# The first reciprocal spread on ScalarE, and nine dummy matmuls for nineteen

## The chip, the cores and the metric

The kernel runs on one core of a Trainium2 chip. A core has five engines that each work through their own queue of instructions in order: TensorE (PE, matrix products; its weight loads are listed as PEld), VectorE (DVE), ScalarE (ACT), GpSimd (POOL) and SyncE (SP), which here only issues DMAs. An instruction that waits holds up everything behind it in its queue. The metric is the device time of one execution in microseconds; smaller is better.

## The reference

Two layers, one after the other. The first is a polynomial-sketch linear attention on q, k and v of 4 batches, 4 heads, 1088 positions and 32 features; the second is a gated feed-forward layer on its output, seen as 4352 tokens of 128 features.

```python
def phi(x):                                  # r = 8, so 64 features
    a = einsum('rd,bhsd->bhsr', S1, x)
    b = einsum('rd,bhsd->bhsr', S2, x)
    return einsum('bhsi,bhsj->bhsij', a, b).reshape(..., r * r)
q_p, k_p = phi(q), phi(k)
kv  = einsum('bhsf,bhsd->bhfd', k_p, v)
z   = sum(k_p, axis=2)
num = einsum('bhsf,bhfd->bhsd', q_p, kv)
den = einsum('bhsf,bhf->bhs', q_p, z)[..., None] + 1e-06
x   = (num / den) in the layout [tokens, heads * features]
out = (relu(x @ w_gate) * (x @ w_val)) @ w_out      # 128 -> 1536 -> 128
```

## The kernel before

The program is a list of operations (`P.add(engine, name, function, inputs)`), made by classes: `K` for k and v of one batch, `First` for the first 512 columns of q of batch 0, `Q` for the other pieces of q, and `F` for one unit of the feed-forward layer. The order is written out by hand: `START` holds a position for each operation, in the order in which the operations were added, and `Plan.run` issues them sorted by it. Each engine thus gets its own queue in that order, and waits only where an input is not ready or a buffer (a PSUM bank by `BANKS`) is not free. `WARM` names operations ahead of which some dummy matmuls are put into PE's queue, 128x128 products of a tile of zeros into PSUM bank 7 (L1007 in the profile).

Batch 0 is worked first so that feed-forward units can start early. For it, `First` handles q in two halves, y = 0 and 1, with a shortcut for the division: the denominator of each (position, head) is built on its own, and its reciprocal is laid out transposed so that it can be multiplied onto the numerator when that leaves PSUM. The steps of one half, with the lines of the profile:

- `f bw` (L672, DVE) multiplies the two factors of the denominator into fbw, `f red` (L614, DVE) sums them, `f rd` (L616, DVE) takes the reciprocal into frd, 8 values per partition.
- `f rx` (L618, DVE in the kernel before) copies each of those 8 values 32 times, 128x8 to 128x256 in fp32, into frx.
- `f rT` (L679, PE) transposes frx by two products with an identity, `f rTe` (L623, ACT) copies the result from PSUM to frT.
- `f phi` (L687, POOL) makes the q features, `f tr` (L696, PE) transposes them, `f pt` (L633, ACT) copies them to fpt, `f num` (L700, PE) multiplies them with bd, the masked kv sum.
- `f xd` (L707, DVE) multiplies numerator and frT into xT, which is what the feed-forward units read.

Around them stand, in the same queues: `kphi` (L534, DVE or POOL), the k features; `kv` (L559, PE) with its evacuation `kve` (L565, DVE) into bd; `w` (L519, PE) with `wc` (L523, ACT); `L` (L379, ACT), a small copy; `cw` (L311, ACT), the casts of the first third of the three weight matrices, that of the gate weights, `cw g0`, first; `qt1 0 4` (L979, DVE), a transpose of the rest of q of batch 0; `gate` (L385, ACT), a one-element cast whose end lets SP issue the loads of the next batches (`ld k1`, L389, first); and on POOL the DMA issues for the other thirds of the weights (L305).

In issue order, the queues near the change are these. DVE: f rd 0, f bw 1, f rx 0, f red 1, f rd 1, kphi 0 6, f rx 1, qt1 0 4, kve 0, f xd 0. ACT: L, cw g0, f rTe 0, wc 0, f pt 0, gate, cw v0, f pt 1, f rTe 1. PE: f csk 1, nineteen dummies, f rT 0, kv 0 0, w 0, f tr 0, four more kv, f rT 1, f tr 1, f num 0, then a score product of the next piece, f num 1 and the first units. POOL: f phi 0, the loads wg2 and wg1, f phi 1, the loads wv2 and wv1.

A feed-forward unit is two products of xT with gate and value weights (L908, PE), a relu out of PSUM (L913, ACT), their product (L923, DVE, or L917 on ACT and L928 on POOL), and the product with the output weights (L936, PE).

Of the kernel before, what the change touches and what calls it, by code (L numbers as in the profile page):

```python
# [27 lines left out]
FILL = 'DVE'  # L28
RINGS = [['ld s1', 'ld s2', 'ld k01', 'ld v000', 'ld v001', 'ld v002', 'ld v003', 'ld v010', 'ld v011', 'ld v012', 'ld v013'], ['mz', 'kt1 0 0'], ['fills', 'kt1 0 0'], ['zero', 'fills'], ['ld k00', 'ld q00', 'table'], ['vc 0 0', 'gate'], ['zero', 'mz'], ['zero', 'sel'], ['zero', 'masks'], ['id32', 's1r', 'ld wg1', 'ld wv1'], ['kphi 0 8', 'ld wo1', 'ld wg2', 'ld wv2', 'ld wo2'], ['ld v013', 'ld wg0', 'ld wv0', 'ld q01'], ['ld wv0', 'ld k1']]
Q0E = 'ACT'  # L30
RXE = 'DVE'
START = [
# [67 lines left out]
]  # L100
WARM = {34: 29, 63: 2, 143: 14, 147: 1, 152: 19}


class Lease:
# [15 lines left out]
class Plan:  # L120
# [10 lines left out]
    def run(self, warm):  # L131
        assert not START or len(START) == len(self.ops)
        order = sorted(self.ops, key=lambda o: (START[o.seq] if START else 0, o.seq))
        for o in order:
            if o.seq in WARM:
                warm(WARM[o.seq])
            o.fn()
# [3 lines left out]
def kernel(  # L141
# [37 lines left out]
    def sb(shape, dt, name):  # L179
        return const.tile(shape, dt, name=name)  # L180

    P = Plan()

    def bank(l, i=0):
        return PS[:, l.banks[i]]
# [393 lines left out]
    cp = {"ACT": nc.scalar.copy, "DVE": nc.vector.tensor_copy, "POOL": nc.gpsimd.tensor_copy}  # L579

    class First:


        def __init__(self, kk, qt1):
            self.kk, n = kk, 4
            self.n = n
            self.ab = sb([128, 2, n, 2, 16], FP32, "fab")
            self.aT = sb([128, n * 128], FP32, "faT")
            self.bw = fbw
            self.dn, self.rd = sb([128, n * H], FP32, "fdn"), sb([128, n * H], FP32, "frd")  # L590
            self.rx = sb([128, n, H, D], FP32, "frx")
            self.rT = sb([128, n * 128], FP32, "frT")
            self.qp = sb([128, n, 2, 128], FP16, "fqp")
            self.pt = sb([128, n, 2, 128], FP16, "fpt")
            rts, t2s = [], []
            for y in range(2):
                la = Lease(P, 2)
                s1 = P.add("PE", f"f sk {y}", lambda y=y, la=la: self.sk(la, y), [qt1[y], ws_op],
                           take=[la])
                t2 = P.add("DVE", f"f t2 {y}", lambda y=y, la=la: self.t2(la, y), [s1],  # L600
                           drop=[la])
                t2s.append(t2)
                lat, lc, lr = Lease(P), Lease(P), Lease(P)
                at = P.add("PE", f"f aT {y}", lambda y=y, l=lat: self.at(l, y), [qt1[y], s1r_op],
                           take=[lat])
                ate = P.add("ACT", f"f aTe {y}", lambda y=y, l=lat: nc.scalar.copy(
                    out=self.aT[:, 256 * y:256 * y + 256], in_=bank(l)[:, 0:256]), [at, ftab],
                    drop=[lat])
                cs = P.add("PE", f"f csk {y}", lambda y=y, l=lc: self.csk(l, y),
                           [kk.zc_op, ate], take=[lc])  # L610
                o1 = P.add("DVE", f"f bw {y}", lambda y=y, l=lc: self.mul(l, y), [t2, cs, f2],
                           drop=[lc])
                h = slice(2 * H * y, 2 * H * y + 2 * H)
                o2 = P.add("DVE", f"f red {y}", lambda h=h: nc.vector.tensor_reduce(  # L614
                    out=self.dn[:, h], in_=self.bw[:, h], axis=AX.X, op=ALU.add), [o1])
                o3 = P.add("DVE", f"f rd {y}", lambda h=h: nc.vector.reciprocal(  # L616
                    out=self.rd[:, h], in_=self.dn[:, h]), [o2])
                rx = P.add(RXE, f"f rx {y}", lambda h=h, y=y: cp[RXE](  # L618
                    out=self.rx[:, 2 * y:2 * y + 2].rearrange("p x h d -> p (x h) d"),
                    in_=self.rd[:, h, None].to_broadcast([128, 2 * H, D])), [o3])  # L620
                rt = P.add("PE", f"f rT {y}", lambda y=y, l=lr: self.rt(l, y), [rx, fid32],
                           take=[lr])
                rts.append(P.add("ACT", f"f rTe {y}", lambda y=y, l=lr: nc.scalar.copy(  # L623
                    out=self.rT[:, 256 * y:256 * y + 256], in_=bank(l)[:, 0:256]), [rt],
                    drop=[lr]))
            self.x_ops = []
            for y in range(2):
                x = slice(2 * y, 2 * y + 2)
                lt, ln = Lease(P), Lease(P)
                phi = P.add("POOL", f"f phi {y}", lambda x=x: self.phi(x), [t2s[y]])  # L630
                tr = P.add("PE", f"f tr {y}", lambda x=x, lt=lt: self.tr(lt, x), [phi, fident],
                           take=[lt])
                pt = P.add("ACT", f"f pt {y}", lambda x=x, lt=lt: nc.scalar.copy(  # L633
                    out=self.pt[:, x].rearrange("f x g t -> f (x g t)"),
                    in_=bank(lt).bitcast(FP16)[:, 0:512]), [tr], drop=[lt])
                num = P.add("PE", f"f num {y}", lambda x=x, ln=ln: self.num(ln, x),
                            [pt, kk.kve], take=[ln])
                self.x_ops.append(P.add(
                    "DVE", f"f xd {y}", lambda y=y, ln=ln: self.xd(ln, y), [num, rts[y]], drop=[ln]))
# [405 lines left out]
```

## Time and profile before

| | |
|---|---|
| median of 3 runs | 105.07 us (104.68 to 108.16) |
| the profiled execution's own time | 104.74 us |
| its span, first to last instruction | 103.0 us |
| mean granted PE clock | 0.994 of full speed |
| PE / DVE / ACT / POOL busy | 97.0 / 85.7 / 82.3 / 60.5 us |
| dummy matmuls (L1007) | 65, of which 19 ahead of the first transposes |

All times in a trace are counted from the span's start. A line of the timeline gives start, length, engine, source line, operation, output <- input with shape and count, and in brackets how long the engine had stood idle before and what ended that. Neighbouring instructions of one group are merged into one line, whose length is from the first start to the last end. A line of the chain gives start, length and what. A row of a group of one tile gives shortest, median and longest duration in ns, then the first and last start.

### The profile page before, as it was taken

The numbers are of one execution on the slowest core, as the hardware profiler recorded it, in microseconds if no ns is written. First come the engines' busy times: TensorE is split into PE (matmuls) and PEld (weight loads), VectorE is DVE, ScalarE is ACT, GpSimd is POOL, SyncE is SP. The second block draws the span as 40 slices with busy tenths as digits, with TensorE's granted clock in tenths as the row PEclk, the third lists the DMA queues.
The fourth block names the chain that finished last, engine by engine and source line by source line (L and its number), as shares of the span: only waits on it lengthen the run. The fifth ranks groups of instructions, "written<-read, shape, count | busy, mean of one in ns | idle before, by whom it ended". The sixth has DMA issues, their size and how long they took to land.

```text
span 103.0 us, 3182 instructions
## 1 busy us (share of the span) xinstructions
PE 97.0 (94%) x1233; PEld 70.2 (68%) x1233; DVE 85.7 (83%) x191; ACT 82.3 (80%) x165; POOL 60.5 (59%) x71
## 2 busy tenths in 40 slices
PE   6999999987999999999999999999999999999950
PEld 6978889845779865556675666656676666678930
DVE  4587969999999898999999887998969895986740
ACT  3437289999797776999988898788998999899920
POOL 2029955978999999995994987108800030264400
PEclk9999999999999999999999999999999999999997
DMA  2988689999994495205530040420513423004131
GB/s 55 350 215 309 101 136 317 354 287 250 227 265 97 118 86 127 54 16 159 149 87 10 0 102 6 102 51 0 127 33 78 108 51 76 6 0 107 46 102 51
DMA packets 14800, 12.40 MB, mean 120 GB/s; under 512 B 8257, under 2 KB 12353, under 8 KB 14785
## 3 DMA queue, kind: packets, MB, share of 16 engines
q1 hardware_dynamic: 13392, 10.70, 40.3%
q0 software_dynamic: 864, 0.79, 5.3%
q10 hardware_dynamic: 528, 0.72, 2.3%
q8 instruction: 9, 0.15, 0.6%
q14 instruction: 7, 0.05, 0.2%
HBM read 9.05 MB, written 2.23 MB: 110 GB/s over the span
## 4 chain that ended last, share of the span: by engine, by line
PE 83%; DVE 11%; issue 1%; ACT 0%; DVEq 0%; POOL 0%
PE ps L908 39%; PE ps L936 22%; PE ps L1007 5%; DVE ht L923 5%; PE ps L559 2%; PE ps L772 2%; PE ps L840 2%; PE ps L492 2%; PE ps L506 2%; DVE kT L483 2%; PE ps L679 1%; PE ps L519 1%; PE ps L666 1%; PE ps L658 1%; DVE frx L618 1%
## 5 line engine op out<-in xcount | busy, mean ns | idle before, releaser
L923 DVE TENSOR_TENSOR ht<-g_sb,ps 128x512 f16<-128x512 f16 (+1 forms) x88 | 55.7, 671 | 7.5 <-PE ps L908 5.1
L913 ACT ACTIVATE g_sb<-ps 128x512 f16<-128x512 f32 x102 | 55.4, 606 | 6.6 <-PE ps L908 6.1
L936 PEld LDWEIGHTS <-ht 128*128 128x128 f16 x408 | 28.2, 98 | 11.1 <-issue 1.8
L908 PE MATMUL ps<-xT,wv 128*128 128x512 f16 (+1 forms) x132 | 35.6, 332 | 0.1
L936 PE MATMUL ps<-wo,ht 128*128 128x128 f16 x408 | 34.6, 219 | 0.0
L908 PE MATMUL ps<-xT,wg 128*128 128x512 f16 (+1 forms) x132 | 34.4, 331 | 0.0
L928 POOL TENSOR_TENSOR ht<-g_sb,v_sb 128x512 f16<-128x512 f16 x15 | 17.2, 1157 | 18.0 <-ACT g_sb L913 14.2
L908 PEld LDWEIGHTS <-wg 128*128 128x128 f16 x132 | 14.1, 114 | 4.3 <-issue 0.8
L534 POOL TENSOR_TENSOR kp<-kab 128x512 f16<-128x512 f32 (+2 forms) x14 | 15.6, 1132 | 2.2 <-DVE kab L498 2.2
L908 PEld LDWEIGHTS <-wv 128*128 128x128 f16 x132 | 13.8, 115 | 4.3 <-issue 1.4
L813 POOL TENSOR_TENSOR qqp<-qan,qabc 128x1024 f16<-128x1024 f32 (+1 forms) x9 | 14.9, 1660 | 0.4
L917 ACT CAST v_sb<-ps 128x512 f16<-128x512 f32 x15 | 9.2, 615 | 0.3
L807 POOL TENSOR_TENSOR qan<-qabc,qrd 128x128 f32<-128x128 f32 (+1 forms) x9 | 3.4, 372 | 7.8 <-DVE qrd L803 7.8
L1007 PE MATMUL ps<-zero 128*128 128x128 f16 x65 | 6.6, 280 | 1.0 <-DVE zero L287 1.0
L1007 PEld LDWEIGHTS <-zero 128*128 128x128 f16 x65 | 5.8, 132 | 1.3 <-DVE zero L287 1.0
L785 DVE STREAM_TRANSPOSE qabc<-ps 128x128 f32<-128x128 f32 (+1 forms) x12 | 5.5, 493 | 0.5 <-PE ps L772 0.4
L979 DVE STREAM_TRANSPOSE qT<-q_sb 128x544 f32<-128x544 f32 (+2 forms) x9 | 5.8, 656 | 0.0
L943 ACT ACTIVATE o_sb<-ps 128x512 f32<-128x512 f32 (+1 forms) x10 | 5.2, 520 | 0.7 <-PE ps L936 0.6
L793 POOL TENSOR_TENSOR bw<-qabc 128x128 f32<-128x128 f32 (+1 forms) x9 | 3.6, 408 | 3.6 <-DVE qabc L785 3.5
L853 ACT CAST xT<-ps 128x512 f16<-128x512 f32 (+1 forms) x9 | 4.8, 535 | 0.6 <-PE ps L840 0.4
L483 DVE STREAM_TRANSPOSE kT<-k_sb 128x544 f32<-128x544 f32 x6 | 4.2, 719 | 0.0
L548 ACT CAST v<-v 128x576 f16<-128x576 f32 x6 | 4.0, 692 | 0.1
(92 smaller groups left out, 78.4 us busy)
## 6 DMA issues: line engine op xcount, KB each, us to landing
k_sb<-in_k_dram SPq DMA_DIRECT2D x3, 544.0 KB
q_sb<-in_q_dram SPq DMA_DIRECT2D x3, 544.0 KB, 10.6
out_dram<-o_sb SPq DMA_DIRECT2D x22, 64.0 KB, 1.7
v<-in_v_dram SPq DMA_DIRECT2D x6, 144.0 KB, 10.0
v<-in_v_dram SPq DMA_DIRECT2D x6, 128.0 KB, 7.8
out_dram<-o_sb SPq DMA_DIRECT2D x16, 32.0 KB, 2.1
v<-in_v_dram SPq DMA_DIRECT2D x6, 64.0 KB, 3.3
k_sb<-in_k_dram SPq DMA_DIRECT2D x1, 288.0 KB, 4.3
```

The costliest lines, as they stand in the source:

```text
L483: nc.vector.transpose(self.kT[:, r], k_sb[self.b][:, r])
L534: eng.tensor_tensor(out=self.kp[:, lo:hi].rearrange("p x g (i a c) -> p (x g i) a c", i=2, a=R), in0=a[:, :, :, None].to_broadcast([128, n ...
L785: nc.vector.transpose(self.abc[:, lo:lo + m, 2 * i2:2 * i2 + 2].rearrange("p x h f -> p h x f"), pair(ls[i2])[:, :, lo * 32:(lo + m) * 32] ...
L813: nc.gpsimd.tensor_tensor(out=self.qp[:, lo:hi].rearrange("p x g (i a c) -> p (x g i) a c", i=2, a=R), in0=self.an[:, lo * H:hi * H, :, No ...
L908: nc.tensor.matmul(bank(l)[:, y * self.W:(y + 1) * self.W], w[:, j // 4, :, j % 4], x, start=True, stop=True, skip_group_check=True)
L913: nc.scalar.activation(out=self.gs, in_=bank(l), func=ACTF.Relu)
L917: nc.scalar.copy(out=self.vs, in_=bank(l))
L923: nc.vector.tensor_tensor(out=self.ht[:, t], in0=self.gs[:, t], in1=bank(l)[:, t], op=ALU.mult)
L928: nc.gpsimd.tensor_tensor(out=self.ht, in0=self.gs, in1=self.vs, op=ALU.mult)
L936: nc.tensor.matmul(o[:, s], self.ht[:, i * 128:(i + 1) * 128], wo[:, j // 4, j % 4], start=(j == 0 and s == 0), stop=(j == NJ - 1), skip_g ...
L979: nc.vector.transpose(qT[b][:, lo:hi], q_sb[b][:, lo:hi])
L1007: nc.tensor.matmul(PS[:, 7, 0:128], zero, zero, start=True, stop=True, skip_group_check=True)
```

## The change

The first of the two `f rx` copies, y = 0, is given to ACT; the second stays on DVE. In the issue order it takes the place just ahead of `cw g0` on ACT's queue; the positions between its new and its old place each move back by one. Ahead of `f rT 0` stand nine dummies in place of nineteen. The computation is the same.

```diff
-RXE = 'DVE'
+RXE = ['ACT', 'DVE']
 START = [ ...
-    2, 4, 1, 8, 6, 43, 10, 12, 13, 15, 17, 22, 28, 31, 3, 9, 0, 14, 34, 64, 40, 89, 20, 103, 71,
-    93, 51, 66, 87, 125, ...
+    2, 4, 1, 8, 6, 43, 10, 12, 13, 15, 17, 22, 28, 31, 3, 9, 0, 14, 34, 65, 40, 89, 20, 103, 71,
+    93, 51, 67, 87, 125, ...
...
-    35, 42, 48, 54, 58, 60, 63, 67, 69, 76, 57, 62, 38, 44, 59, 65, 68, ...
+    35, 42, 48, 54, 58, 60, 63, 64, 69, 76, 57, 62, 38, 44, 59, 66, 68, ...
...
-WARM = {34: 29, 63: 2, 143: 14, 147: 1, 152: 19}
+WARM = {34: 29, 63: 2, 143: 14, 147: 1, 152: 9}
...
-                rx = P.add(RXE, f"f rx {y}", lambda h=h, y=y: cp[RXE](
+                rx = P.add(RXE[y], f"f rx {y}", lambda h=h, y=y: cp[RXE[y]](
                     out=self.rx[:, 2 * y:2 * y + 2].rearrange("p x h d -> p (x h) d"),
                     in_=self.rd[:, h, None].to_broadcast([128, 2 * H, D])), [o3])
```

Of the four moved positions, 64 to 65 is `cw g0`, 66 to 67 is `ld wg2` on POOL, 65 to 66 is `f bw 1`, and 67 to 64 is `f rx 0`. The order within every other queue stays as it was.

4 rows, old and new, of the table START are left out of this document.

## The prediction

> **What bounds the kernel now.** The page comes first: the busy shares, and the chain of work that ended last.
>
> ```profile
> span 103.0 us, 3182 instructions
> PE 97.0 (94%) x1233; PEld 70.2 (68%) x1233; DVE 85.7 (83%) x191; ACT 82.3 (80%) x165; POOL 60.5 (59%) x71
> PE 83%; DVE 11%; issue 1%; ACT 0%; DVEq 0%; POOL 0%
> ```
>
> TensorE (PE) is busy for 94% of the span and carries 83% of the chain. That is an average over stages, so the second view is the table by stretches (columns: length, then busy time of PE, PEld, DVE, ACT and POOL with instruction counts, the granted PE clock, the DMA share, GB/s).
>
> ```profile
> 11.00:12.00 1.00, 1.00 (x19) 0.86 (x16) 0.99 (x2) 0.47 (x1) 0.99 (x3) 1.00 0.60 112
> ...
> 16.00:18.00 2.00, 2.00 (x20) 1.93 (x19) 1.85 (x9) 1.87 (x5) 1.30 (x4) 1.00 1.03 350
> 24.00:27.00 3.00, 2.56 (x62) 1.63 (x61) 3.00 (x8) 2.93 (x8) 2.92 (x3) 1.00 1.10 223
> 27.00:40.00 13.00, 13.00 (x234) 10.28 (x218) 12.35 (x25) 10.38 (x21) 12.58 (x13) 1.00 0.78 156
> 80.00:95.00 15.00, 15.00 (x149) 10.65 (x148) 12.14 (x20) 14.41 (x29) 4.58 (x4) 1.00 0.23 57
> ```
>
> From 27 us on PE has no gap: what is left to do there takes its own time, and a stage that starts earlier ends earlier by as much. Between 16 and 27 us DVE is as good as full. The change sits at 11 to 12 us, ahead of both, where PE looks full only because dummies fill it. The third view is the chain in order of time.
>
> ```profile
> 11.01 0.22 DVE fbw L672
> 11.23 0.96 DVE frx L618
> 12.23 0.71 PE ps L679 x4
> ...
> 14.02 0.64 PE ps L679 x4
> ...
> 14.89 0.25 PE ps L700 x2
> 15.23 0.40 DVE xT L707
> ```
>
> The copy that is moved (L618, 0.96 us of it) is on the path that sets the end; the dummies beside it are not. Behind it the PE queue runs through without a break to the product that is the first block of xT. The last view is the timeline around it.
>
> ```profile
> 9.82 0.26 ACT L379 COPY L<-ps 128x128 f32<-128x128 f32 x1
> ...
> 10.81 1.12 POOL L305 DMA_DIRECT2D wg<-in_moe_w_gate_dram  x2
> 10.81 0.16 DVE L616 RECIPROCAL frd<-fdn 128x8 f32<-128x8 f32 x1
> 10.81 1.23 PE L1007 MATMUL ps<-zero 128*128 128x128 f16 x19
> 11.01 0.22 DVE L672 TENSOR_TENSOR fbw<-fab,ps 128x64 f32<-128x64 f32 x1
> 11.15 1.03 DVE L618 COPY frx<-frd 128x256 f32<-128x256 f32 x1
> 11.53 0.62 ACT L311 CAST wg<-qabc 128x512 f16<-128x512 f32 x1 [1.45 <-DMA qabc<-in_moe_w_gate_dram]
> 11.94 1.17 POOL L687 TENSOR_TENSOR fqp<-fab 128x512 f16<-128x512 f32 x1
> 12.10 0.21 DVE L614 TENSOR_REDUCE fdn<-fbw 128x8 f32<-128x72 f32 x1
> 12.23 0.52 PEld L679 LDWEIGHTS ps<-id,frx 128*128 128x128 f32 x4 [0.38 <-DVE frx L618]
> ...
> 12.47 0.64 DVE L534 TENSOR_TENSOR kp<-kab,ps 128x512 f16<-128x512 f32 x1
> ...
> 12.98 0.37 ACT L623 COPY frT<-ps 128x256 f32<-128x256 f32 x1 [0.84 <-PE ps L679]
> ...
> 13.02 0.29 DVE L618 COPY frx<-frd 128x256 f32<-128x256 f32 x1
> 13.06 1.12 POOL L305 DMA_DIRECT2D wv<-in_moe_w_val_dram  x2
> 13.23 0.77 DVE L979 STREAM_TRANSPOSE qT<-q_sb 128x576 f32<-128x576 f32 x1
> ```
>
> Two things are to be seen. The two copies of L618 have the same shape, and the first takes 1.03 us, the second 0.29. The first lies under POOL's two DMA issues (10.81 to 11.93) and ends 0.25 us after them. And ACT stands idle from 10.08 to 11.53, waiting for the gate weights to land.
>
> **The change part by part.** *The copy on ACT.* Its input is ready when the reciprocal ends, 10.81 + 0.16 = 10.97. For the hand-over I take the 0.05 us by which PE followed the copy in the trace (11.15 + 1.03 = 12.18, and 12.23), so it starts at 11.02. The trace has no ACT copy of this source; the two rows below and the 1.03 us bound it.
>
> ```profile
> L606 ACT COPY faT<-ps x2: 372/372/373, 8.1 to 8.6; 128x256 f32<-128x256 f32 x2
> 14.12 0.61 ACT L311 CAST wv<-qabc 128x512 f16<-128x512 f32 x1
> ```
>
> ACT copies 128x256 from PSUM in 0.37 us; the same copy took 1.03 on DVE. I take 0.37, since the ACT cast at 11.53 lay partly under POOL's DMA issue and took the 0.62 us that its fellow at 14.12 takes. The copy ends at 11.39, inside ACT's idle time: the cast of the gate weights, which waits for its DMA, still starts at 11.53, and the insertion costs nothing. At 1.03 us the copy would end at 12.05 and that cast at 12.67.
>
> *The dummies.* Nineteen take 1.23 us; nine take 9/19 of it, 0.58, and end at 11.39. With nineteen the queue would hold the transposes until 12.04, so the move alone would bring 0.19 us; the two edits need each other. With the hand-over of 0.05 behind ACT's 11.39 the transposes start at 11.44, call it 11.45. **At this place 12.23 - 11.45 = 0.78 us is won.**
>
> *What ACT does next.* The evacuation at L623 started 0.75 us after the transposes, so at 12.20, behind the cast's end at 12.15: it moves by the same 0.78, as do the copies behind it.
>
> *What DVE does next.* Without the copy the second half's reduction follows its product as the first half's did, about 0.25 us after 11.01: 11.26 for 12.10. The reciprocal, the kp product and the second copy keep their distances (12.47 and 13.02 less 12.10), so the product ends at 12.27 and the second copy asks at 12.18. That is where the forecast divides. In the trace of before this copy met POOL's multiply (11.94 to 13.11) only in its last 0.09 us; now it would meet 0.9 us of it. Either it runs at once, 0.29 us to 12.47, or it waits as the first one did and ends 0.25 after POOL, at 13.11 + 0.25 = 13.36. I take the second, because the only copy of this form that began well inside a POOL operation was held to its end.
>
> The Trainium skill, SBUF — State Buffer, section "SBUF: two separate sides", says that DVE and GpSimd share one port pair under an exclusive lock, and that an fp32 copy from SBUF to SBUF asks for it and is shut out for the whole instruction of the other. The 1.03 us beside 0.29 agree with it for DMA issues; no run yet shows it for the multiply. By that rule POOL, first at 11.94, keeps the second copy out, and the time is that of the forecast; without it, that of the first rival.
>
> *How far that takes the gain back.* The rows that follow, from the timeline, carry the next steps; the last is the time from issue to landing of the two wv loads.
>
> ```profile
> 13.95 0.71 PE L679 MATMUL ps<-id,frx 128*128 128x128 f32 x4
> 14.03 0.18 ACT L385 CAST k_sb<-zero 1x1 f32<-1x1 f16 x1
> 14.06 0.29 DVE L565 TENSOR_TENSOR bd<-ps,maskg 128x128 f16<-128x128 f32 x1
> 14.24 0.80 SPq L389 DMA_DIRECT2D k_sb<-in_k_dram  x2
> 14.82 0.30 PE L700 MATMUL ps<-fpt,bd 128*64 128x256 f16 x2
> 17.64 0.38 PE L908 MATMUL ps<-xT,wv 128*128 128x256 f16 x2
> DMA to landing us min/median/max: 3.0/3.3/3.7
> ```
>
> From the first transposes to the second PE had 13.95 - 12.23 = 1.72 us of work without a gap: if the second copy is free, the second ones would start at 13.17; held, at 13.41. Behind the held copy the DVE queue is where it was: the qT transpose about 13.28 to 14.05, then the evacuation of kv, 14.06 before, now 14.07, 0.29 long, to 14.36. With 0.05 the products of L700 can start at 14.41; before it was PE's own queue that let them start at 14.82.
>
> So **0.41 us are left at L700**, and xT, the first gate product and all behind them move by that. The sum is made against the profiled execution, 104.74 us of its own (span 103.0 and 1.74 around it): 104.74 - 0.41 = 104.33. The runs shown have their median at 105.07, 0.33 above it, and the lowest at 104.68; I give **104.35** and keep the scatter for the range.
>
> *What the moved ACT queue triggers.* The tiny cast at 14.03 opens SP's queue: k of the next batch is issued at 14.24 behind it, and would be at 13.46. These 544 KB then meet the last two weight loads of POOL's queue, issued at 13.06 and after and landed 3.0 to 3.7 us later (last row). The first is needed by PE at 17.64, at 17.23 when all is 0.41 earlier; it lands by 13.06 + 3.7 = 16.76, so 0.47 us are in hand.
>
> **Rivals.** *The second copy runs free.* Then the qT transpose behind it waits only for its q.
>
> ```profile
> 7.60 0.44 SPq L265 DMA_DIRECT2D q_sb<-in_q_dram  x1
> q_sb<-in_q_dram SPq DMA_DIRECT2D x1, 288.0 KB, 5.3
> ```
>
> That lands at 7.60 + 5.3 = 12.9; the transpose ends at 12.9 + 0.77 = 13.67 and the kv evacuation about 0.3 later, at 13.97. PE's order is then the limit throughout: L700 at 14.82 - 0.78 = 14.04. Time 103.96. For it: the 0.29 us. Against it: that copy had all but outlived POOL's work.
>
> *The gain is lost on the way.* Either the ACT copy takes 1.03 us like its fellow (transposes at 12.10, 0.13 won, 104.61), or the earlier k pushes the weight load back by the whole 0.78 us that it comes forward, to 17.54: PE then stands 0.31 us, 0.10 is left, 104.64. Call both 104.6.
>
> *Slower than before.* The same load waits out the whole transfer of k: 544 KB at the 350 GB/s of the stretch from 16 to 18 us are 1.56 us, it lands at 18.32, and PE's queue stands there 0.68 us longer than before: 105.42. It decides from a push of 0.88 us (past 17.64). Against it: k was already under way from 14.24 while these loads were landing.
>
> *The clock falls.* Ten dummies less could let the granted clock drop; if PE ran at half of it from the first transposes to the end of the first L700 (12.23 to 15.12 before), those 2.9 us would cost 2.9 more, about 107.2. Against it: the gap ahead of the transposes shrinks (0.2 us before, about 0.06 after), and the clock is 1.00 in every stretch above. The Trainium skill, TensorE: Matmul & The Clock Gate, Part 1, puts an idle window of about 3.4 us ahead of a drop, which the gap is far from.
>
> **How the numbers follow.** Forecast 0.48 (104.35); second copy free 0.22 (103.96); gain lost 0.16 (104.6); slower by the load 0.10 (105.4); clock 0.04 (107). Below: the lowest run less the larger gain is 104.68 - 0.78 = 103.90; 0.2 for half the scatter of 104.68 to 105.07 gives 103.7. Above: the slower case, 105.4, taken to 105.5, which is also the median shown with its own scatter on top. Within 2% (2.1 us) is what a measurement of this kernel can't tell from no change: all cases but the clock lie in it. Faster by over 2% would need 2.1 us where 0.78 is the most: 0.02. Slower by over 2%: the clock, and a little for a median that falls among runs like the 108.16 shown, 0.06. Same: 0.92.
>
> **What would show it.** Right: an ACT copy into frx at about 11.0 of 0.37 us, the gate cast still at 11.5, nine dummies ending at 11.4, L679 first at 11.45, the second L618 drawn out to about 1.1 us and ended at 13.3, L700 at 14.4, PE without a gap from 26.6. A second L618 of 0.3 us with L700 at 14.0 speaks for the first rival; an ACT copy near 1 us, or a PE wait before the products with wv at 17 us, for the second and third; a granted clock under 1.00 at 12 to 15 us for the last. The prediction is wrong if stages behind 16 us, which I let move as one, change their waits.

## The result, and the profile after

| | before | after |
|---|---|---|
| median of 20 runs | 104.94 us (104.28 to 110.98) | 104.92 us (103.57 to 108.52) |
| ratio of undisturbed executions, 95% | | 0.9935 (0.9906 to 0.9965) |
| the profiled execution's own time | 104.74 us | 103.83 us |
| its span | 103.0 us | 102.1 us |

By the ratio 0.65% is won, 0.68 us of 104.74 (0.37 to 0.98): faster beyond its interval, and within the 2% called the same. The medians show none of it: the ratio keeps of each kernel only the executions within 1.5% of its own fastest, ten of twenty of the changed kernel and fifteen of the kernel before; with one line of 105.84 us for both, fifteen of each, the means are 104.53 and 104.84 us. That would be a gain of 0.3%, so its size leans on where the line is drawn. A second set of the changed kernel, at the end of the experiments, gave 0.9914. The forecast was 104.35 in a range of 103.7 to 105.5, with 0.41 us won.

The page of the changed kernel, its busy shares and its chain:

```profile
span 102.1 us, 3160 instructions
PE 96.4 (94%) x1223; PEld 69.4 (68%) x1223; DVE 85.4 (84%) x190; ACT 82.5 (81%) x166; POOL 60.3 (59%) x71
PE 85%; DVE 9%; issue 1%; ACT 0%; POOL 0%; DVEq 0%
```

Ten matmuls and one DVE instruction fewer, one ACT instruction more; DVE's share of the chain fell from 11% to 9%. The timeline around the change:

```profile
10.68 0.16 DVE L616 RECIPROCAL frd<-fdn 128x8 f32<-128x8 f32 x1
10.68 1.12 POOL L305 DMA_DIRECT2D wg<-in_moe_w_gate_dram  x2
10.68 0.67 PE L1007 MATMUL ps<-zero 128*128 128x128 f16 x9
10.87 0.40 ACT L618 COPY frx<-frd 128x256 f32<-128x256 f32 x1 [0.90 <-DVE frd L616]
...
11.18 0.61 ACT L311 CAST wg<-qabc 128x512 f16<-128x512 f32 x1
11.33 0.52 PEld L679 LDWEIGHTS ps<-id,frx 128*128 128x128 f32 x4 [0.15 <-ACT frx L618]
...
11.81 1.09 POOL L687 TENSOR_TENSOR fqp<-fab 128x512 f16<-128x512 f32 x1
...
12.08 0.98 DVE L618 COPY frx<-frd 128x256 f32<-128x256 f32 x1
...
12.98 0.76 DVE L979 STREAM_TRANSPOSE qT<-q_sb 128x576 f32<-128x576 f32 x1
...
13.12 0.71 PE L679 MATMUL ps<-id,frx 128*128 128x128 f32 x4
...
13.33 0.80 SPq L389 DMA_DIRECT2D k_sb<-in_k_dram  x2
...
13.68 0.24 DVE L565 TENSOR_TENSOR bd<-ps,maskg 128x128 f16<-128x128 f32 x1
...
13.98 0.30 PE L700 MATMUL ps<-fpt,bd 128*64 128x256 f16 x2
```

The copy runs on ACT in 0.40 us. The second one, left on DVE, is now the long one: 0.98 us under POOL's multiply, where it took 0.29 before. Read all of this against the start of the first reciprocal (L616), since the first loads land a little differently in every execution, and with them everything moves: the reciprocal starts at 10.81 before and at 10.68 after.

| us after the first reciprocal's start | before | forecast | after |
|---|---|---|---|
| first L679 | 1.42 | 0.64 | 0.65 |
| second L618, start to end | 2.21 to 2.50 | 1.37 to 2.55 | 1.40 to 2.39 |
| second L679 | 3.14 | 2.60 | 2.44 |
| kv evacuation L565, start | 3.25 | 3.26 | 3.00 |
| first L700 | 4.01 | 3.60 | 3.30 |

0.71 us are won at L700. Behind it the kernel is what it was: from the start of L700 to the end of the span 103.0 - 14.82 = 88.2 us before and 102.1 - 13.98 = 88.1 after. So 0.91 us between the two profiled executions is 0.13 of an earlier reciprocal, 0.71 of the change and 0.07 of the rest. The table by stretches of the changed kernel (columns as in the prediction) shows the same PE stage without a gap from 27 us on:

```profile
12.00:13.00 1.00, 1.00 (x25) 0.94 (x22) 1.00 (x3) 0.88 (x3) 1.00 (x2) 1.00 0.86 109
24.00:27.00 3.00, 2.62 (x60) 1.89 (x60) 2.95 (x7) 2.82 (x7) 3.00 (x4) 1.00 1.05 237
27.00:40.00 13.00, 12.99 (x217) 10.09 (x215) 12.16 (x25) 9.77 (x20) 12.73 (x13) 1.00 0.74 147
```

One wait is new. The view of the tile wv in the changed kernel has its two loads landed 4.1 to 5.5 us after their issue, not 3.0 to 3.7:

```profile
DMA to landing us min/median/max: 4.1/4.8/5.5
```

and in the timeline PE stood for one of them:

```profile
16.98 0.14 PEld L908 LDWEIGHTS <-wv 128*128 128x128 f16 x2 [0.28 <-DMA wv<-in_moe_w_val_dram]
```

It cost nothing at the end. DVE's first product of a unit (ht, L923) started 2.91 us after L700 in both profiles (17.73 - 14.82, and 16.89 - 13.98), and four of them later the first transpose of k (L483) started 5.34 us after L700 in both (20.16 - 14.82, and 19.32 - 13.98).

### The profile page after: what moved, and what is told of

Same layout as the page of the kernel before. It is cut to its first block, busy times and chain, and to the rows that moved or that the text cites. A ratio compares the mean times of both kernels' runs of the same rounds, so it can differ in the third digit from the quotient of the medians.

```text
span 102.1 us, 3160 instructions
## 1 busy us (share of the span) xinstructions
PE 96.4 (94%) x1223; PEld 69.4 (68%) x1223; DVE 85.4 (84%) x190; ACT 82.5 (81%) x166; POOL 60.3 (59%) x71
## 4 chain that ended last, share of the span: by engine, by line
PE 85%; DVE 9%; issue 1%; ACT 0%; POOL 0%; DVEq 0%
PE ps L908 39%; PE ps L936 23%; PE ps L1007 5%; DVE ht L923 4%; PE ps L559 2%; PE ps L772 2%; PE ps L840 2%; PE ps L492 2%; PE ps L506 2%; DVE kT L483 2%; PE ps L679 1%; PE ps L519 1%; PE ps L658 1%; PE ps L666 1%; DVE qabc L785 1%
## 5 line engine op out<-in xcount | busy, mean ns | idle before, releaser
L923 DVE TENSOR_TENSOR ht<-g_sb,ps 128x512 f16<-128x512 f16 (+1 forms) x88 | 55.6, 671 | 7.5 <-PE ps L908 4.9
L928 POOL TENSOR_TENSOR ht<-g_sb,v_sb 128x512 f16<-128x512 f16 x15 | 17.2, 1156 | 17.9 <-ACT g_sb L913 14.2
L1007 PE MATMUL ps<-zero 128*128 128x128 f16 x55 | 5.9, 287 | 1.0 <-DVE zero L287 1.0
L1007 PEld LDWEIGHTS <-zero 128*128 128x128 f16 x55 | 5.1, 136 | 1.3 <-DVE zero L287 1.0
L483 DVE STREAM_TRANSPOSE kT<-k_sb 128x544 f32<-128x544 f32 x6 | 4.2, 719 | 0.0
```

What stands on the lines that cost most here:

```text
L483: nc.vector.transpose(self.kT[:, r], k_sb[self.b][:, r])
L923: nc.vector.tensor_tensor(out=self.ht[:, t], in0=self.gs[:, t], in1=bank(l)[:, t], op=ALU.mult)
L928: nc.gpsimd.tensor_tensor(out=self.ht, in0=self.gs, in1=self.vs, op=ALU.mult)
L1007: nc.tensor.matmul(PS[:, 7, 0:128], zero, zero, start=True, stop=True, skip_group_check=True)
```

## Experiments

Theory: the first copy was long because DVE was kept out while POOL issued its loads; the dummies were the next bound; the stages behind move as one. A time such as R + 0.65 is in us after the start of the first reciprocal of that execution. The ratios are to the kernel before on the same chip.

**The move alone.** Nineteen dummies again.

```diff
-WARM = {..., 147: 1, 152: 9}
+WARM = {..., 147: 1, 152: 19}
```

> The first copy on ACT, but nineteen dummies as before. Theory (the copy was held behind POOL, and the dummies would hold the transposes next): the ACT copy again 0.40 us, but the first L679 starts only when the dummies end, 1.23 us after the reciprocal's start (1.42 in the kernel before, 0.65 in the changed one); about 0.2 us is won, ratio to the kernel before about 0.998. Rival (the move alone makes the gain): first L679 about 0.65 us after the reciprocal's start, ratio 0.993 to 0.994.

From the timeline of this kernel, the reciprocal, the dummies, the first transposes and the first numerator product:

```profile
10.45 0.16 DVE L616 RECIPROCAL frd<-fdn 128x8 f32<-128x8 f32 x1
10.45 1.22 PE L1007 MATMUL ps<-zero 128*128 128x128 f16 x19
11.51 0.66 PE L679 MATMUL ps<-id,frx 128*128 128x128 f32 x4
...
14.04 0.30 PE L700 MATMUL ps<-fpt,bd 128*64 128x256 f16 x2
```

Ratio 0.9949 (0.9921 to 0.9976); first L679 at R + 1.06, first L700 at R + 3.59. The dummies do bound it, but less than expected (a ratio of about 0.998, first L679 at R + 1.23): they let PE go 0.16 us earlier than the end that the timeline gives them (1.22), so that modelled end is not when the queue is free. Of 0.71 us at L700 the move brings 0.42 (4.01 to 3.59), the shorter row of dummies the other 0.29, by one profile of each kernel. The ratios don't show the second part: 0.9949 here and 0.9935 for both edits lie within each other's intervals.

**The dummies alone.** Nine dummies, both copies on DVE.

```diff
-WARM = {..., 147: 1, 152: 19}
+WARM = {..., 147: 1, 152: 9}
```

> Nine dummies, but both copies on DVE. Theory: the copy still ends with POOL's two DMA issues, 1.37 us after the reciprocal's start, so the first L679 starts where it did (1.42) and PE idles about 0.8 us ahead of it; granted clock stays 1.00 at 11 to 15 us; ratio 1.000 (0.997 to 1.003). Rival one (fewer dummies make the gain): ratio 0.9935. Rival two (the idle time lowers the clock): a clock under 1.00 between 11 and 15 us and 1 to 3 us more.

The table by stretches of this kernel (the granted clock is the third number from the end; the first reciprocal is at 12.85 in this execution):

```profile
13.00:14.00 1.00, 0.52 (x10) 0.34 (x7) 0.96 (x3) 0.00 (x0) 0.99 (x1) 1.00 1.04 143
14.00:16.00 2.00, 1.72 (x13) 1.66 (x14) 1.97 (x6) 0.40 (x2) 1.16 (x3) 0.63 0.62 83
16.00:18.00 2.00, 2.00 (x22) 1.82 (x20) 0.34 (x2) 1.35 (x4) 0.00 (x0) 0.51 0.64 101
18.00:20.00 2.00, 1.99 (x48) 1.45 (x48) 1.19 (x5) 1.51 (x4) 0.16 (x1) 1.00 0.93 313
```

and from its timeline POOL's multiply, the first copy and the first transposes:

```profile
13.01 1.06 POOL L687 TENSOR_TENSOR fqp<-fab 128x512 f16<-128x512 f32 x1 [0.42 <-DVE frd L616]
...
13.19 1.03 DVE L618 COPY frx<-frd 128x256 f32<-128x256 f32 x1
...
14.28 1.02 PE L679 MATMUL ps<-id,frx 128*128 128x128 f32 x4 [0.76 <-DVE frx L618]
```

Ratio 1.0127 (1.0072 to 1.0182): **slower**, by 1.3 us. The theory's 1.000 fell, and its second rival held: PE idles 0.76 us, and the granted clock is at half from about 14.5 to 17.9. The mean clock was 0.984 in five of the six executions, as one such stretch would make it (half of 3.4 us in 104). It was 0.968 in the sixth, the profiled one, which had a stretch at half clock from 8 to 11 us too, behind an earlier wait for q. In this execution the first copy lay under POOL's multiply (13.01 to 14.07) and no longer under its DMA issues, and was as long. The dummies, then, were not idle filling: with them the clock was kept through the wait for the copy. A second profile of the same kernel began with q landed so late that its clock was at half long before, and says nothing on this:

> Nine dummies with both copies on DVE once more, for the granted clock in another execution. Theory (the idle 0.76 us ahead of the first L679 costs the clock each time): a stretch of about 3.4 us at 0.5 that begins within 1 us of the first L679. Rival (the first look was an execution with a late start): clock 1.00 from 11 to 18 us.

**No dummies at all** in the changed kernel.

```diff
-WARM = {..., 147: 1, 152: 9}
+WARM = {..., 147: 1}
```

> The changed kernel with no dummies ahead of the first transposes: PE is idle from the end of the products L666 to the first L679, about 0.65 us where nine dummies lay. Theory (the dummies earn their place by keeping the granted clock; an idle time of 0.76 us lost it in the kernel with nine dummies and the copy on DVE): a granted clock of 0.5 for a stretch of about 3.4 us between 11 and 18 us in at least some executions, ratio 1.005 to 1.01. Rival (a shorter gap is harmless once the copy is early): the clock stays at 1.00, ratio 0.9935.

From the timeline of this kernel, the cast of v on ACT and the first transposes:

```profile
10.52 0.73 ACT L552 CAST v<-v 128x640 f16<-128x640 f32 x1 [1.55 <-DMA v<-in_v_dram]
11.77 0.49 PE L679 MATMUL ps<-id,frx 128*128 128x128 f32 x2 [0.97 <-ACT frx L618]
```

and two rows of its table by stretches:

```profile
13.00:14.00 1.00, 1.00 (x18) 0.91 (x15) 0.70 (x2) 0.76 (x4) 0.91 (x2) 0.50 0.86 135
14.00:16.00 2.00, 2.00 (x12) 1.50 (x12) 0.29 (x1) 0.75 (x3) 0.00 (x0) 0.50 1.05 151
```

Both answers, by execution. In three of six the clock was 0.997 or more and the time as good as with nine (ratio 0.9881, 0.9816 to 0.9946, among these alone); in the other three it was 0.960 to 0.984, at 106.1 to 106.3 us. The profiled one is of the latter: here v landed late, the cast on ACT (L552) ahead of the copy was late with it, PE idled 0.97 us and the clock was at half from about 12.6 to 16. So the kernel without dummies can be as good and can lose its clock. That the copy was early in the three good executions, and that nine dummies would have covered the others, is argued; no trace of this set shows it.

**The copy stays on DVE, and reads PSUM.** Nine dummies, kernel before otherwise; the first reciprocal is written to a free bank.

```diff
-out=self.rd[:, h]                    # f rd
+out=self.rd[:, h] if y else PS[:, 1, 0:2 * H]
-in_=self.rd[:, h, None]              # f rx
+in_=(self.rd[:, h] if y else PS[:, 1, 0:2 * H])[:, :, None]
```

> Both copies stay on DVE and nine dummies, but the first reciprocal is written to PSUM and the first copy reads it there. Theory (what made the first copy long is that DVE's copy from SBUF to SBUF is kept out while POOL is at work): read from PSUM it takes 0.3 to 0.4 us, the first L679 starts about 0.75 us after the reciprocal's start, and the gain is nearly that of the change, ratio about 0.994. Rival (DVE's queue has to be relieved of the copy, or the copy is long for another reason): still about 1.0 us, ratio 1.000.

From the timeline of this kernel, POOL's issues, the reciprocal, the first copy, the first transposes and the first numerator product:

```profile
10.65 1.12 POOL L305 DMA_DIRECT2D wg<-in_moe_w_gate_dram  x2
...
10.76 0.21 DVE L616 RECIPROCAL ps<-fdn 128x8 f32<-128x8 f32 x1
...
11.01 0.42 DVE L618 COPY frx<-ps 128x256 f32<-128x256 f32 x1
11.49 0.52 PEld L679 LDWEIGHTS ps<-id,frx 128*128 128x128 f32 x4 [0.34 <-DVE frx L618]
...
14.07 0.30 PE L700 MATMUL ps<-fpt,bd 128*64 128x256 f16 x2
```

Ratio 0.9946 (0.9900 to 0.9992), first L679 at R + 0.73, L700 at R + 3.31. Same engine, same shape, same place under the same two DMA issues: 0.42 us from PSUM where it took 1.03 from SBUF. What made it long is thus the read from SBUF while POOL is at work, not DVE's load, and ACT was one way around it of two.

**The second copy earlier.** In the changed kernel, ahead of the kp product on DVE.

```diff
+START[162] = 71.5        # f rx 1, was 77; kphi 0 6 is at 72
```

> The changed kernel with the second copy on DVE ahead of the kp product, so that it asks some 0.5 us earlier, inside POOL's DMA issues (about 0.9 us after the first reciprocal's start). Theory (DVE is let in when POOL goes from one kind of work to the next, as the first copy was before): it ends about 0.2 us after the DMA issues, 0.45 us long, POOL's multiply ends 0.1 to 0.2 us later, and the ratio is that of the changed kernel, 0.993. Variant of the theory (held to the end of the multiply): 1.5 us long, the kp product behind it late by 1.0, the products of L559 wait for that and L700 starts about 0.5 us later than in the changed kernel, ratio about 0.998. Rival (a copy that is merely slow beside POOL): about 1.0 us from wherever it starts.

From the timeline of this kernel, POOL's issues, the second copy, POOL's multiply, PE's wait for a wv load, and DVE's wait behind it:

```profile
11.12 1.12 POOL L305 DMA_DIRECT2D wg<-in_moe_w_gate_dram  x2
...
12.05 0.41 DVE L618 COPY frx<-frd 128x256 f32<-128x256 f32 x1
...
12.25 1.14 POOL L687 TENSOR_TENSOR fqp<-fab 128x512 f16<-128x512 f32 x1
17.85 0.15 PEld L908 LDWEIGHTS <-wv 128*128 128x128 f16 x2 [0.76 <-DMA wv<-in_moe_w_val_dram]
...
18.37 1.88 DVE L923 TENSOR_TENSOR ht<-g_sb,ps 128x512 f16<-128x512 f16 x3 [0.44 <-PE ps L908]
```

The copy is let in between: it asks at 12.05, ends 0.22 us after POOL's issues (12.24), takes 0.41, and POOL's multiply is 1.14 long for 1.09. It is not merely slow beside POOL, it is kept out until POOL turns to its next work. L700 came at R + 3.27, no later than in the changed kernel. And yet the ratio was 0.9998 (0.9964 to 1.0031), where 0.993 was expected. The wv loads landed 4.5 to 6.8 us after issue, PE's weight loads stood 0.76 us for the first and 0.92 for the second, and DVE's second ht waited 0.44 us for PE. From L700 to the end this execution took 102.9 - 14.37 = 88.5 us, 0.4 more than the changed kernel's.

**The same, with SP's queue opened later.** The cast that opens it is put behind the cast of the value weights.

```diff
+START[162] = 71.5; START[40] = 89.5      # f rx 1; gate, was 88, cw v0 is at 89
```

> The kernel with the second copy ahead of the kp product (which was not faster than the kernel before, with PE waiting 0.76 us for a wv load), and the tiny cast that opens SP's queue behind the cast of the value weights. Theory (its gain of 0.74 us at L700 was eaten by wv loads that landed 4.5 to 6.8 us after their issue, behind the earlier k): with k issued about 0.5 us later they land in 3 to 4 us, PE waits less than 0.1 us for them, and the ratio comes to 0.993 to 0.995. Rival (the loss lies elsewhere): PE no longer waits there, ratio still 0.999 to 1.001.

From the timeline of this kernel, the two waits for loads:

```profile
19.74 0.69 PEld L908 LDWEIGHTS <-wv 128*128 128x128 f16 x7 [0.21 <-DMA wv<-in_moe_w_val_dram]
20.39 1.37 DVE L483 STREAM_TRANSPOSE kT<-k_sb 128x544 f32<-128x544 f32 x2 [0.53 <-DMA k_sb<-in_k_dram]
```

Ratio 0.9883 (0.9817 to 0.9948), on another chip and from four executions: faster than the kernel before again. But the trace doesn't bear the theory out. The wv loads landed in 2.8 to 5.7 us and not in 3 to 4, PE's weight load stood 0.21 us, and DVE stood 0.53 us for k. From L700 to the end this execution took 103.1 - 14.44 = 88.7 us, no less than without the later opening. In these two traces one side's loads or the other's are late; that the order of the loads decides over the gain is argued, not shown.

**The later opening alone**, in the changed kernel.

```diff
+START[40] = 89.5
```

> The changed kernel with the tiny cast that opens SP's queue behind the cast of the value weights, so that k of the next batch is issued about 0.6 us later. Theory (the wait of 0.28 us for a weight load at 17 us comes from k's earlier transfer, and is paid from slack): the wv loads land in 3 to 4 us again for 4.1 to 5.5, the wait is gone, and the ratio stays at that of the changed kernel, 0.993 to 0.994. Rival (that wait costs): ratio 0.991. Rival (loads of k, q and v are what the middle needs): slower, 0.996 or more.

From the timeline of this kernel, the cast of v, the copy behind it and the first transposes:

```profile
10.45 0.73 ACT L552 CAST v<-v 128x640 f16<-128x640 f32 x1 [1.70 <-DMA v<-in_v_dram]
11.24 0.41 ACT L618 COPY frx<-frd 128x256 f32<-128x256 f32 x1
11.70 0.49 PE L679 MATMUL ps<-id,frx 128*128 128x128 f32 x2 [0.61 <-ACT frx L618]
```

and from the view of its tile wv, the time to landing:

```profile
DMA to landing us min/median/max: 3.4/3.4/3.5
```

Ratio 0.9938 (0.9900 to 0.9977). The wv loads landed in 3.4 to 3.5 us, the wait of 0.28 is gone, and the time is that of the changed kernel within the interval: the wait was paid from slack. From L700 to the end it is 102.4 - 14.28 = 88.1 us, as with the wait. The trace shows a cost of the move that I had not named: on ACT the copy stands behind the cast of v (L552), which waits for v's load. Here v was late, the copy began 0.82 us after the reciprocal's start, not 0.19, and L679 came at R + 1.28.

**Both copies on ACT.**

```diff
-RXE = ['ACT', 'DVE']
+RXE = ['ACT', 'ACT']
+START[162] = 75.5        # f rx 1, behind cw g0 on ACT
```

> The changed kernel with the second copy on ACT too, right behind the cast of the gate weights. Theory (the second copy is held 0.7 us on DVE, but PE's own queue hides all but about 0.07 us of that): ACT copies of 0.40 us, the evacuation L623 about 0.1 us later, the second L679 at PE's own pace (1.72 us after the first), L700 at most 0.1 us earlier than in the changed kernel against the reciprocal's start; ratio to the kernel before 0.992 to 0.994. Rival (the held copy still costs, as the 0.3 us that the prediction took off for it): ratio 0.990 or 0.991.

From the timeline of this kernel, where the reciprocal starts at 11.63, the second copy and the kv evacuation:

```profile
12.65 0.40 ACT L618 COPY frx<-frd 128x256 f32<-128x256 f32 x1
...
14.10 0.29 DVE L565 TENSOR_TENSOR bd<-ps,maskg 128x128 f16<-128x128 f32 x1 [0.27 <-PE ps L559]
```

Ratio 0.9948 (0.9906 to 0.9990). L700 at R + 3.23 (14.86), 0.07 us earlier than in the changed kernel: that is what the held copy costs. DVE's evacuation now waits 0.27 us for PE's kv products (L559), so PE's queue and not DVE's sets this place. From L700 to the end this execution took 103.3 - 14.86 = 88.4 us, 0.3 more than the changed kernel's; where those are lost is not settled.

**The changed kernel beside these**, on two chips.

> The changed kernel once more, beside the two others on the same chip: ratio 0.9935 within 0.003, the second copy 0.9 to 1.0 us long and the first L679 0.65 us after the reciprocal's start again.

> The changed kernel beside these on the same chip: ratio 0.9935 within 0.003; the span less the start of L700 is 88.1 us as in its first profile (88.12) and in that of the kernel before (88.18).

The first gave 0.9914 (0.9871 to 0.9957); its profiled execution took 315.5 us of span and is not read, so only the ratio of what was expected is answered. The second gave no ratio, and from L700 to the end its profiled execution took 109.0 - 20.17 = 88.8 us and not 88.1. The timeline shows what disturbed it:

```profile
6.86 0.45 DVE L979 STREAM_TRANSPOSE qT<-q_sb 128x256 f32<-128x256 f32 x1 [2.05 <-DMA q_sb<-in_q_dram]
7.79 0.35 PE L646 MATMUL ps<-qT,wS 64*32 64x64 f32 x16 [1.80 <-DVE qT L979]
```

and one row of its table by stretches:

```profile
10.00:22.00 12.00, 12.00 (x135) 9.83 (x134) 5.28 (x18) 5.88 (x15) 5.60 (x10) 0.50 0.76 186
```

q landed 2 us later than in the profile of before, where its transpose began at 4.95; PE stood 1.80 us and then worked at half clock until about 22 us.

Two further lines of that timeline don't fit the theory of the DMA issues, POOL's issues of the wv loads and the second copy:

```profile
15.36 1.13 POOL L305 DMA_DIRECT2D wv<-in_moe_w_val_dram  x2
...
16.05 0.29 DVE L618 COPY frx<-frd 128x256 f32<-128x256 f32 x1
```

The copy lies wholly inside these issues (15.36 to 16.49) and still takes 0.29 us. Behind them POOL has nothing to do until 21.98, while the wg issues that held a copy, in the kernel before and in the kernel with the second copy earlier, have POOL's multiply right behind them. Whether the issue itself or the multiply queued behind it keeps DVE out is not settled by these runs; that the multiply does while it runs is shown (13.01 and 13.19 in the run of the dummies alone, 11.81 and 12.08 in the changed kernel).

## Why the prediction was right, and where it missed

The direction, the range and most of the mechanism held; the size was short, 0.41 us for 0.71 at L700 (0.68 by the ratio, whose interval includes 0.41).

- *The copy on ACT*: 0.37 forecast, 0.40 measured, start 0.21 after the reciprocal's start forecast, 0.19 measured. Inserted at no cost ahead of the gate cast: right, though in this execution the cast followed the copy at once (11.18), its weights having landed. What was missing is the v cast ahead of it, shown by the later opening alone.
- *The dummies*: the first L679 at R + 0.64, measured 0.65. "The move alone would bring 0.19 us" was wrong: 0.36 at L679, since nineteen dummies hold the queue 1.06 us and not 1.23. That the two edits need each other held on one side only: the dummies alone are slower by 1.3%, while the move alone brings 0.42 of the 0.71 us at L700, and its ratio can't be told from that of both.
- *The second copy*: held, as forecast; asked at R + 1.40 (1.37), ended at 2.39 (2.55), as POOL's multiply took 1.09 and not 1.17 and the copy's tail was 0.17 us and not 0.25. The Trainium skill's rule on the shared ports (SBUF — State Buffer, "SBUF: two separate sides") thus holds for the multiply too, and the first rival, the copy running free, is out. For the DMA issues the 0.29 us of the copy at 16.05, in the last trace of the changed kernel, stands against it.
- *How far that takes the gain back* is **the step that was mis-sized**: 0.37 us were taken off, and the held copy cost 0.07 (L700 at R + 3.30, against 3.23 with both copies on ACT). The working let the kv evacuation set L700, at R + 3.60. The runs show PE's queue in its place: in the eight traces with a clock of 1.00 there (both kernels and six of the experiments), L700 starts 0.86 or 0.87 us after the second L679 (13.95 and 14.82 before, 13.12 and 13.98 after). By that distance the forecast's own second L679, at R + 2.60, would have given R + 3.47; the other 0.17 us come with the held copy, which ended 0.16 us earlier than forecast.
- *Why the evacuation did not bind*: it started at R + 3.00 and not 3.26, and took 0.24 us and not 0.29, so it ended 0.06 us ahead of L700. Of its earlier start 0.16 us is the copy's. The rest is that it starts as the transpose ahead of it drains, 0.06 us before that one's end, where in the kernel before it came 0.06 us behind (the working took 0.02). That fits a wait for PE's kv products in the kernel before, which the run with both copies on ACT shows in the open; in the trace of before itself it isn't recorded, and is only argued.
- *The stages behind move as one*: right, 88.2 and 88.1 us from L700 to the end.
- *The moved ACT queue and wv*: the loads did come later, by up to 1.8 us (5.5 for 3.7), past the 0.47 us in hand. PE's wait of 0.28 us at 17 us is the sign that was named for the second and third rivals, and a changed wait behind 16 us was named as a sign of being wrong. That it cost nothing was not foreseen and is luck as far as the prediction goes. The rival of the late load is real, though not in this kernel: with the second copy earlier, a wait of PE for wv and of DVE behind it goes with 0.4 us lost behind L700.
- *The clock*: 1.00 at 11 to 18 us, as forecast. The reason given, that the gap is far from 3.4 us, was too easy: half clock followed 0.76 us of idle time in the run of the dummies alone, so the margin was some tenths of a us.

## What to carry to other kernels

When one copy takes three times as long as its twin, look at what the engine beside it does in that time; here another engine and a source in PSUM each took the wait away. Dummies that fill a wait belong to that wait: left in whole they held PE until R + 1.06, where nine let it go at R + 0.65, and cut while the wait stayed they cost the clock. When a forecast takes a place over from the trace of before, ask what set it there: here that of the kv evacuation was taken from DVE's queue, and PE's queue set the time. And read two executions against an event close ahead of the change (here the reciprocal), not against the span's start: the first loads put that event anywhere from 10.42 to 15.13 us in the traces read here, a wider spread than the change is worth.

## What the runs showed of the hardware

- An fp32 copy of 128x256 on DVE from SBUF to SBUF took 0.29 us when POOL's multiply had 0.09 us left, 0.98 to 1.03 when it asked 0.2 to 0.3 us after that multiply had begun, and 1.03 under two DMA issues with the multiply right behind them. The same copy from PSUM took 0.42 under such issues, and on ACT 0.40. Under the wg issues it was let in as POOL went on to the multiply and not between the two issues; in one trace it ran inside the wv issues in 0.29 us.
- The granted clock went to half for about 3.4 us after an idle time of PE of 0.76 us, and of 0.97 us, ahead of four fp32 products; after 0.61 us in one execution it did not.
- The two wv loads of POOL's queue landed within 3.0 to 3.7 us in the six traces where k was issued on SP's queue 1.2 us or more behind the first of them (13.06 and 14.24 before). In the six where k came 0.4 to 0.9 us behind (12.83 and 13.33 after), the later of the two landed 5.0 to 6.8 us after issue.
